# Spectral mixer and MLP on one core: where two transposes, one split, the rest columns, the pair sums and one bias are done

## The chip, the cores and the metric

The kernel runs on one core of one Trainium2 chip. The metric is device microseconds (us) of one execution of the whole program; three executions of the kernel before gave 2691.61, 2695.22 and 2697.30 us, so the median is 2695.22 us. The engines are named as in the profile: PE (TensorE, matmuls), PEld (its weight loads), DVE (VectorE), ACT (ScalarE), POOL (GpSimd) and SP (SyncE, which here only issues DMAs). Each engine executes its own instructions in the order of the program; engines wait for one another by semaphores.

## The reference, cut to what matters

`x` is 2048 x 576, `w1` 576 x 4608 and `w2` 4608 x 576, all float32. Two kinds of layer alternate, twice each.

```python
def A(y):                        # spectral mixing, y = layernorm(x)
    a = y @ dft_hid_re.T
    b = y @ dft_hid_im.T
    return dft_seq_re @ a - dft_seq_im @ b

def B(y):                        # MLP; normalizes y once more inside
    h = gelu(layernorm(y) @ w1 + b1)
    return h @ w2 + b2

x = x + A(layernorm(x))
x = x + B(layernorm(x))
x = x + A(layernorm(x))
x = x + B(layernorm(x))
```

## The kernel before, in words

All matmuls are float32 products made of three reduced-precision passes (`PASSES`): each operand is split into a high part (a copy by ACT into type fp32r) and a low part (operand minus high part, by DVE). `split` (L201 for ACT, L198 for DVE, since every subtraction is recorded at the helper `sub`) does both; names with `high` and `low` do one each. The big products go through a seven-product scheme over 2 x 2 blocks (`ORDER` lists the seven), which needs sums and differences of blocks beforehand.

One layer pair has these stages, in this order.

- **Sequence stage** (`Sequence.run`, from L698). The seq-DFT is done first, on 16 output tiles of 128 rows. The two *plain tiles* come first (`first_mms`, eight block pairs). The other 14 go through the *main loop*: 98 steps of 24 matmuls with 288 columns, seven to a tile. Step n makes, ahead of time, the low part for step n+2 (`low`, DVE) and the high part for step n+3 (`high`, L647, ACT); `sums` makes the next tile's block sums on DVE. After a step `post` combines its PSUM bank. Finished tiles (`uv`, 128 x 1152) are transposed in 32 x 32 blocks on DVE (`turned`, L205) and stored to `uv_mid` in DRAM. In the first layer, `pump` puts pieces of the preparation of `w1` between the steps: loads `in_w`, high parts at L278/L279 (ACT), low parts (DVE), sums (POOL).
- `first_post` (L602) copies the four PSUM banks of a plain tile to SBUF (L606, ACT), transposes it (DVE) and issues its store from ACT's queue (L609), so ACT stands until the transpose is done. For tile 0 this comes straight after `first_mms`, ahead of the main loop's first low part; for tile 1 after step 1.
- During the seven steps of the last tile `Hidden.begin` (L756) prepares the next stage: it issues the loads of the hidden-DFT matrix `dh` (nine blocks) and of the first `uv` tiles (four DMAs each), in the first layer splits the nine blocks (`high_d` L821, `low_d`), and at n == 5 splits the first `uv` tile (`turn(0)`), behind blocks 3 to 5.
- **Hidden stage** (`hidden`, from L871), twice per layer, for 8 tiles each. Tile n is 54 matmuls (9 blocks x 3 passes x 2 halves). Then DVE adds the result to the residual tile (L195), takes its statistics (L223 to L226), and POOL turns these into a scale and an offset (L229, L232, L233: the *moments*). At the start of tile n+1 ACT splits the `uv` tile n+2 (L201) and normalizes tile n (L252) into a buffer `t8` shared by two tiles, and POOL adds the bias `b2` to the residual tile (L195). After every second tile a pair is complete. `rests` copies the last 32 columns of four blocks, three times each, into `es` (L917, three POOL copies). Behind the matmuls of the even tiles 2, 4 and 6 `turn_blocks` transposes a pair on PE: eight 128 x 128 transposes (L931) and four from `es` (L934), copied out of PSUM by ACT (L935, L936). In the next odd tile `turn_sums` splits three blocks (`parts`, L944 and L198) and makes four block sums of 128 x 384 (on POOL for the first two pairs, on DVE for the third); `turn_parts` then splits the four sums.
- **MLP stage** (`mlp`): products with `w1`, gelu, products with `w2`, by the same scheme.

Nothing reorders the work: each engine's queue is the order in which the Python code calls it. SP issues most DMAs, one after the other.

## Time and profile before

| | us |
|---|---|
| median of three executions | 2695.22 (2691.61 to 2697.30) |
| the profiled execution | 2693.01 |
| its span, first to last instruction | 2691.1 |
| PE busy in the span | 2644.4 (98%) |
| ACT busy | 1099.5 (41%) |
| DVE busy | 1819.4 (68%) |
| POOL busy | 850.6 (32%) |

Between the span and the time of the profiled execution lie 1.9 us. A row of the profile's list of groups or of its timeline gives a source line, engine, operation, `out<-in`, shapes of output and input, a count, busy time, and in brackets or behind the last bar the time the engine had been idle before it and what ended that. A row of the timeline merges neighbouring instructions of one line and engine under the shape of the first. All subtractions stand under L198 and all additions under L195.

### The profile page before, as it was taken

How to read it: one execution, taken by the hardware profiler on the slowest of the kernel's cores; microseconds unless marked ns; L12 is line 12 of the kernel's file. 1: busy time of each engine (PE TensorE's matmuls, PEld its weight loads, DVE VectorE, ACT ScalarE, POOL GpSimd, SP SyncE). 2: the span in 40 equal slices, each digit the busy share in tenths (PEclk: the TensorE clock that was granted, in tenths of full speed). 3: DMA queues.
4: the chain of work that ended last, by engine and by line, in shares of the span. 5: the costliest groups of instructions: out<-in, count | busy, mean ns of one | idle time of the engine just before them, and what ended most of it. 6: DMA issues, size and time to landing. Idle time of an engine off the chain costs nothing. (4 is left out here: it accounts for less than half of the span.)

```text
span 2691.1 us, 44720 instructions
## 1 busy us (share of the span) xinstructions
PE 2644.4 (98%) x17252; PEld 2479.6 (92%) x17252; DVE 1819.4 (68%) x2515; ACT 1099.5 (41%) x1773; POOL 850.6 (32%) x766
## 2 busy tenths in 40 slices
PE   9999999999999999999999999999999999999998
PEld 9999998888888988998899999988999999899998
DVE  8999976877777565556667776566555556655555
ACT  6555644544453343333344333343333324433332
POOL 5344335434443532222251000143222235322222
PEclk9999999999999999999999999999999999999999
DMA  5677675777778566666453333646666684766664
GB/s 189 238 263 244 238 259 185 258 267 274 266 278 291 162 187 195 195 217 207 156 209 121 121 121 121 204 132 194 195 191 197 193 265 133 206 193 195 192 194 152
DMA packets 223109, 544.90 MB, mean 202 GB/s; under 512 B 23584, under 2 KB 74784, under 8 KB 222752
## 3 DMA queue, kind: packets, MB, share of 16 engines
q1 hardware_dynamic: 209568, 511.94, 60.1%
q10 hardware_dynamic: 13328, 30.09, 2.9%
q8 instruction: 137, 2.24, 0.3%
q14 instruction: 76, 0.62, 0.1%
HBM read 429.87 MB, written 114.72 MB: 202 GB/s over the span
## 5 line engine op out<-in xcount | busy, mean ns | idle before, releaser
L208 PE MATMUL bank<-R 128*128 128x288 f32 (+2 forms) x16972 | 2613.2, 316 | 21.6 <-DVE R L198 6.3
L208 PEld LDWEIGHTS bank<-R 128*128 128x128 f32 x16972 | 2448.2, 189 | 182.4 <-DVE A L195 16.5
L195 DVE TENSOR_TENSOR A<-bank,A 128x576 f32<-128x576 f32 (+3 forms) x808 | 568.5, 710 | 558.2 <-PE bank L208 471.4
L198 POOL TENSOR_TENSOR R<-A,R 128x512 fp32r<-128x512 f32 (+1 forms) x286 | 373.3, 1316 | 904.6 <-ACT R L1233 877.2
L198 DVE TENSOR_TENSOR R<-A,R 128x1024 fp32r<-128x1024 f32 (+10 forms) x539 | 535.0, 1018 | 81.0 <-ACT R L944 30.7
L195 POOL TENSOR_TENSOR A<-A 128x576 f32<-128x576 f32 (+2 forms) x102 | 155.2, 1524 | 542.5 <-ACT A L687 343.9
L198 POOL TENSOR_TENSOR A<-A 128x384 f32<-128x384 f32 (+3 forms) x184 | 229.3, 1249 | 248.1 <-DVE R L198 102.2
L1172 ACT ACTIVATE bank<-bank,b1t 128x512 f32<-128x512 f32 (+1 forms) x224 | 144.9, 647 | 368.7 <-DVE bank L195 242.7
L1233 ACT ACTIVATE R<-A 128x512 fp32r<-128x512 f32 x288 | 177.0, 629 | 273.2 <-DVE A L198 123.7
L647 ACT ACTIVATE R<-A 128x1024 fp32r<-128x1024 f32 x196 | 206.1, 1053 | 120.1 <-PE bank L208 63.2
L195 DVE TENSOR_TENSOR bank<-bank,A 128x512 f32<-128x512 f32 (+1 forms) x228 | 152.2, 670 | 143.5 <-PE bank L208 142.6
L198 DVE TENSOR_TENSOR R<-bank,R 128x512 fp32r<-128x512 f32 x232 | 156.3, 676 | 4.7 <-ACT R L1233 4.2
L198 DVE TENSOR_TENSOR A<-A 128x1024 f32<-128x1024 f32 (+3 forms) x134 | 143.3, 1076 | 4.5
L1199 ACT ACTIVATE A<-bank 128x512 f32<-128x512 f32 (+1 forms) x76 | 43.7, 575 | 229.1 <-PE bank L208 229.0
L1233 ACT ACTIVATE R<-bank 128x512 fp32r<-128x512 f32 x216 | 121.2, 595 | 30.1 <-PE bank L208 30.1
L198 DVE TENSOR_TENSOR A<-bank,A 128x512 f32<-128x512 f32 x144 | 98.0, 681 | 0.0
L1172 ACT ACTIVATE A<-bank,b1t 128x512 f32<-128x512 f32 (+1 forms) x76 | 50.5, 665 | 66.5 <-DVE bank L195 66.5
L278 ACT ACTIVATE R<-A 128x256 fp32r<-128x256 f32 x126 | 52.0, 413 | 59.1 <-DMA w_parts<-R 21.8
L252 ACT ACTIVATE A<-A,moments 128x576 f32<-128x576 f32 x58 | 48.5, 860 | 52.7 <-POOL moments L233 24.6
L279 ACT ACTIVATE R<-A,power,middle 128x128 fp32r<-128x128 f32 x126 | 60.8, 483 | 0.0
L944 ACT ACTIVATE R<-A 128x768 fp32r<-128x768 f32 (+2 forms) x36 | 32.9, 946 | 56.0 <-POOL A L198 55.9
L205 DVE STREAM_TRANSPOSE A<-A 128x1152 f32<-128x1152 f32 x32 | 44.1, 1378 | 10.9 <-ACT A L606 7.6
(64 smaller groups left out, 601.6 us busy)
## 6 DMA issues: line engine op xcount, KB each, us to landing
R<-w_parts SPq DMA_DIRECT2D x504, 320.0 KB, 3.4
R<-w_parts SPq DMA_DIRECT2D x189, 576.0 KB, 3.7
A<-in_cs SPq DMA_DIRECT2D x112, 512.0 KB, 4.1
w_parts<-R SPq DMA_DIRECT2D x63, 576.0 KB, 5.3
w_parts<-R ACTq DMA_DIRECT2D x81, 320.0 KB, 3.6
uv_mid<-A SPq DMA_DIRECT2D x28, 576.0 KB, 3.0
w_parts<-R SPq DMA_DIRECT2D x45, 320.0 KB, 4.3
A<-in_w SPq DMA_DIRECT2D x72, 192.0 KB, 4.5
```

The source lines that it names most:

```text
L195: engine.tensor_tensor(dst, a, b, op=op)
L198: engine.tensor_tensor(dst, a, b, op=OP.subtract)
L205: nc.vector.transpose(block(2 * D), block(2 * D))
L208: nc.tensor.matmul(o, a, b, start=start, stop=stop, skip_group_check=True)
L252: nc.scalar.activation(dst, src, AF.Identity, bias=mv[:, 4:5], scale=mv[:, 3:4])
L278: nc.scalar.activation(t[:, 1:4:2], src[:, 0:3:2], AF.Copy)
L279: nc.scalar.activation(t[:, 2], src[:, 1], AF.Identity, bias=power[:, 2:3], scale=middle)
L647: nc.scalar.activation(self.cells[t, i](2, NP, P)[:, 0], self.source(t, i), AF.Copy)
L944: nc.scalar.activation(y[:, i, 0:3, at], x, AF.Copy)
L1172: nc.scalar.activation(dst, src, AF.Gelu_apprx_tanh, bias=bias(f))
L1199: nc.scalar.activation(up, o, AF.Copy)
L1233: nc.scalar.activation(H[q, k](2, TC)[:, 0], src, AF.Copy)
```

## The change

Five things change; what is computed stays the same.

- The transpose and store of plain tile 0 move from ahead of the main loop to behind step 1, those of tile 1 from behind step 1 to behind step 3 (`first_turn`). The bank copies stay where they were. The buffers involved are reserved later accordingly.
- In `Hidden.begin` the split of the first `uv` tile (`turn(0)`) and the load behind it move ahead of `high_d`/`low_d` of step 5, and the load of the second `uv` tile moves from step 0 to step 2.
- `rests` for the first three pairs is one ACT copy with 384 elements a partition in place of three POOL copies with 128.
- `turn_sums` runs on DVE for all pairs.
- The addition of `b2` (POOL) is recorded at the fifth block of the next tile instead of straight after the normalization.

```diff
@@ first_post
                     nc.scalar.activation(uv[:, i, 1 - j], banks[4 * (1 - t) + 2 * i + j][:, :DH], AF.Copy,
                                          scale=-1.0 if i else 1.0)
+
+        def first_turn(self, t, out):
             turned(out)
             nc.scalar.dma_start(uvd[t], out(2 * D))
+            clock[0] += 1
+            out.free()
@@ post
-            if i == 1:
+            if i == 2:
                 self.out = A.alloc(2 * D)
@@ run
-            outs[0].free()
-            hidden.reserve()
...
                 if n == 1:
+                    self.first_turn(0, outs[0])
+                    hidden.reserve()
                     self.first_post(1, outs[1])
-                    clock[0] += 1
-                    outs[1].free()
+                if n == 3:
+                    self.first_turn(1, outs[1])
@@ Hidden.begin
-            if n == 0:
-                self.load_uv(0)
-                self.load_uv(1)
+            if n in (0, 2):
+                self.load_uv(n // 2)
...
+            if n == 5:
+                drain(self.turn(0, Block(R, self.first_ut, 2 * KH * P)))
+                self.load_uv(2)
             for k in ((), (), (), (), (0, 1, 2), (3, 4, 5), (6, 7, 8))[n]:
                 self.high_d(k)
                 self.low_d(k)
-            if n == 5:
-                drain(self.turn(0, Block(R, self.first_ut, 2 * KH * P)))
-                self.load_uv(2)
@@ norms
                 normalize(z, tile_x, mv)
-                add(nc.gpsimd, tile_x, tile_x, b2t(2, DH))
...
             yield
+            if n < NP - 1:
+                add(nc.gpsimd, tile_x, tile_x, b2t(2, DH))
+            yield
@@ rests
             if j < 3:
-                for r in range(3):
-                    nc.gpsimd.tensor_copy(es(7, 3, 32)[:, :4, r], v[:, 0:4, 2 * P:])
+                nc.scalar.activation(es(7, 3, 32)[:, :4], v[:, 0:4, None, 2 * P:].to_broadcast([P, 4, 3, 32]), AF.Copy)
                 return
@@ turn_sums
-            g = nc.gpsimd if j < 2 else nc.vector
+            g = nc.vector
@@ hidden, loop over the tiles
             if n:
-                drain(turn(n + 1), *ln)
+                drain(turn(n + 1))
+                next(ln)
...
+                if k == 4:
+                    next(ln, None)
...
-            g = norms(n)
-            next(g)
-            ln = [g]
+            ln = norms(n)
+            next(ln)
```

The order of instructions shows it at three places. First DVE's queue in the first layer, from the last low part of the plain tiles (128x4x288) to behind step 1. `R<-A,R 128x1024` is the low part of a main-loop step, `A<-A 128x1024` a block sum, `A<-bank,A` the `post` of step 1. Before:

```order
L198 TENSOR_TENSOR R<-A,R 128x4x288
L205 STREAM_TRANSPOSE A<-A 128x1152
L198 TENSOR_TENSOR R<-A,R 128x1024
L195 TENSOR_TENSOR A<-A 128x1024
L198 TENSOR_TENSOR A<-A 128x1024 x2
L198 TENSOR_TENSOR A<-A 128x2x288
L198 TENSOR_TENSOR R<-A,R 128x1024
L198 TENSOR_TENSOR R<-A,R 128x4x288
L198 TENSOR_TENSOR R<-A,R 128x1024
L198 TENSOR_TENSOR A<-A 128x1024
L198 TENSOR_TENSOR R<-A,R 128x1024
L195 TENSOR_TENSOR A<-bank,A 128x288
```

And in the changed kernel:

```order
L198 TENSOR_TENSOR R<-A,R 128x4x288
L198 TENSOR_TENSOR R<-A,R 128x1024
L195 TENSOR_TENSOR A<-A 128x1024
L198 TENSOR_TENSOR A<-A 128x1024 x2
L198 TENSOR_TENSOR A<-A 128x2x288
L198 TENSOR_TENSOR R<-A,R 128x1024
L198 TENSOR_TENSOR R<-A,R 128x4x288
L198 TENSOR_TENSOR R<-A,R 128x1024
L198 TENSOR_TENSOR A<-A 128x1024
L198 TENSOR_TENSOR R<-A,R 128x1024
L195 TENSOR_TENSOR A<-bank,A 128x288
L205 STREAM_TRANSPOSE A<-A 128x1152
```

The transpose of tile 0 has moved from ahead of the first low part of the main loop to behind the `post` of step 1. Second, POOL's queue in a hidden stage, from the bias addition of tile 1 (`A<-A 128x2x288`) to the copies of the second pair. Before:

```order
L195 TENSOR_TENSOR A<-A 128x2x288
L917 COPY A<-A 128x4x32 x3
L229 TENSOR_TENSOR moments<-moments,power 128x1
L232 TENSOR_TENSOR moments<-moments 128x1
L233 TENSOR_TENSOR moments<-power,moments 128x1
L195 TENSOR_TENSOR A<-A 128x2x288
L198 TENSOR_TENSOR A<-A 128x384 x4
L229 TENSOR_TENSOR moments<-moments,power 128x1
L232 TENSOR_TENSOR moments<-moments 128x1
L233 TENSOR_TENSOR moments<-power,moments 128x1
L195 TENSOR_TENSOR A<-A 128x2x288
L917 COPY A<-A 128x4x32 x3
```

And in the changed kernel:

```order
L195 TENSOR_TENSOR A<-A 128x2x288
L229 TENSOR_TENSOR moments<-moments,power 128x1
L232 TENSOR_TENSOR moments<-moments 128x1
L233 TENSOR_TENSOR moments<-power,moments 128x1
L195 TENSOR_TENSOR A<-A 128x2x288
L229 TENSOR_TENSOR moments<-moments,power 128x1
L232 TENSOR_TENSOR moments<-moments 128x1
L233 TENSOR_TENSOR moments<-power,moments 128x1
L195 TENSOR_TENSOR A<-A 128x2x288
```

The three copies and the four sums are gone from POOL; the bias addition stands where it stood. The copy stands in ACT's queue straight behind the normalization, and the sums in DVE's queue between `parts` and the residual addition of the odd tile. Third, DVE's queue at steps 4 to 6 of the last tile in the first layer: `R<-R 128x576` is a `low_d` of one `dh` block, `R<-A,R 128x1152` the low part of the split of the first `uv` tile. Before:

```order
L198 TENSOR_TENSOR R<-R 128x576 x3
L198 TENSOR_TENSOR R<-A,R 128x3x128
L195 TENSOR_TENSOR A<-bank,A 128x288
L198 TENSOR_TENSOR R<-R 128x576 x3
L198 TENSOR_TENSOR R<-A,R 128x1152
L198 TENSOR_TENSOR R<-A,R 128x3x128
```

And in the changed kernel:

```order
L198 TENSOR_TENSOR R<-R 128x576 x3
L198 TENSOR_TENSOR R<-A,R 128x3x128
L195 TENSOR_TENSOR A<-bank,A 128x288
L198 TENSOR_TENSOR R<-A,R 128x1152
L198 TENSOR_TENSOR R<-R 128x576 x3
L198 TENSOR_TENSOR R<-A,R 128x3x128
```

The split of the `uv` tile now stands ahead of blocks 3 to 5 instead of behind them.

More of the change, by code (lines that the diff above doesn't have):

```diff
@@ L673, in post @@
             b = banks[4 - 4 * (t % 2) + BANK[i]][:, :DH]
-            if i == 1:
+            if i == 2:
                 self.out = A.alloc(2 * D)
-            uv, (p1, p5, p7) = self.out(2, 2, DH), (self.post_tmp(3, DH)[:, k] for k in range(3))
+            p1, p5, p7 = (self.post_tmp(3, DH)[:, k] for k in range(3))
+            uv = self.out(2, 2, DH) if i not in (1, 6) else None
             u = p1
@@ L988, in turn_y @@
             t8s.give(t8.pop(j))
-        ln = []
+        ln = iter(())
         for n in range(NP):
@@ L1034, in hidden @@
         parts(2, slice(0, 4), slice(3, 7), low=False)
-        drain(g)
+        drain(ln)
         for _ in range(2):
```

## The prediction

> **What bounds the kernel now.** PE is busy 98% of the span, so anything to be gained is in its idle time. I read first who made PE wait (columns: who waited, for whom, us in total, times, longest):
>
> ```profile
> PE bank L934 <- POOL A L917: 15.2, 8, 2.5
> PE bank L208 <- DVE R L198: 6.3, 6, 2.4
> PE bank L208 <- DVE A L195: 5.0, 4, 2.0
> PE bank L208 <- ACT R L647: 2.8, 2, 1.4
> ```
>
> The largest row is the change's first target: the four transposes of `es` (L934) waited eight times, twice in each of the four hidden stages, for POOL's rest copies (L917). The L647 row is the first split of the main loop, once per layer.
>
> Next the granted clock, in windows placed around these waits (columns: window, its length, busy us and instructions of PE, PEld, DVE, ACT, POOL, then granted clock, DMA share and GB/s):
>
> ```profile
> 66.30:69.70 3.40, 1.34 (x8) 1.11 (x9) 2.08 (x2) 2.06 (x3) 2.46 (x2) 1.00 0.01 2
> 69.70:73.10 3.40, 3.40 (x16) 3.40 (x16) 2.38 (x2) 3.40 (x6) 0.00 (x0) 0.51 0.02 5
> 421.30:424.70 3.40, 0.90 (x7) 0.64 (x7) 3.23 (x7) 0.02 (x1) 3.30 (x4) 1.00 0.27 74
> 424.70:428.10 3.40, 3.40 (x15) 3.37 (x16) 0.60 (x1) 3.28 (x4) 0.93 (x3) 0.50 0.92 256
> 2247.40:2250.80 3.40, 3.40 (x17) 3.40 (x15) 1.26 (x1) 3.40 (x5) 0.98 (x4) 0.51 1.02 293
> ```
>
> Windows of 3.4 us at half clock follow windows in which PE was busy for only 1.34 or 0.90 us. There are eight half-clock windows, the first and the last shown; four follow a wait at L934, one each first split, one the end of the first sequence stage, and one a wait late in the first layer that this change doesn't touch. Each loses 3.4 x 0.5 = 1.7 us. So a wait of 2 to 2.5 us is paid nearly twice.
>
> **Hidden stages: rests to ACT, sums to DVE, bias later.** These rows are tiles 3 and 4 of the first hidden stage, for PE, POOL, ACT and DVE (start, busy, engine, line; idle before in brackets):
>
> ```profile
> 406.52 14.63 PE L208 MATMUL bank<-R 128*128 128x288 f32 x108
> 420.99 1.21 PE L931 MATMUL bank<-ident,A 128*128 128x128 f32 x8
> 424.70 1.09 PE L934 MATMUL bank<-ident,A 128*96 128x128 f32 x4 [2.50 <-POOL A L917]
> 403.69 1.43 POOL L195 TENSOR_TENSOR A<-A 128x576 f32<-128x576 f32 x1 [0.98 <-ACT A L252]
> 413.65 4.29 POOL L198 TENSOR_TENSOR A<-A 128x384 f32<-128x384 f32 x4 [1.95 <-DVE R L198]
> 417.90 0.56 POOL L229 TENSOR_TENSOR moments<-moments,power 128x1 f32<-128x1 f32 x1
> 418.80 0.19 POOL L233 TENSOR_TENSOR moments<-power,moments 128x1 f32<-128x1 f32 x1
> 421.35 2.59 POOL L195 TENSOR_TENSOR A<-A 128x576 f32<-128x576 f32 x1 [2.35 <-ACT A L252]
> 423.88 0.76 POOL L917 COPY A<-A 128x128 f32<-128x128 f32 x3
> 417.97 1.49 ACT L944 ACTIVATE R<-A 128x1536 fp32r<-128x1536 f32 x1 [7.06 <-POOL A L198]
> 419.37 1.15 ACT L201 ACTIVATE R<-A 128x1152 fp32r<-128x1152 f32 x1
> 420.42 0.85 ACT L252 ACTIVATE A<-A,moments 128x576 f32<-128x576 f32 x1
> 409.04 4.37 DVE L198 TENSOR_TENSOR R<-A,R 128x1152 fp32r<-128x1152 f32 x5 [1.50 <-ACT R L201]
> 413.99 0.76 DVE L195 TENSOR_TENSOR A<-bank,A 128x576 f32<-128x576 f32 x1 [0.58 <-PE bank L208]
> 414.79 0.82 DVE L223 BATCH_NORM_STATS2 moments<-A 128x6 f32<-128x288 f32 x2
> 419.49 3.19 DVE L198 TENSOR_TENSOR R<-A,R 32x512 fp32r<-32x512 f32 x3 [3.46 <-ACT R L944]
> ```
>
> The chain is long: the sums hold POOL to 417.9; the moments of tile 3 stand behind them and end at 418.99; ACT waits 7.06 us for the sums, then splits them (1.49) and the next `uv` tile (1.15) before it normalizes (0.85, to 421.3); POOL adds the bias (2.59) and only then copies (0.76), to 424.6. PE had begun L931 at 420.99.
>
> The two operations that take over stand elsewhere in the trace (list of groups by shape; mean ns behind the busy time):
>
> ```profile
> L944 ACT ACTIVATE R<-A 128x384 fp32r<-128x384 f32 x12 | 6.1, 511 | 0.0
> L198 DVE TENSOR_TENSOR A<-A 128x384 f32<-128x384 f32 x16 | 8.9, 558 | 0.9
> ```
>
> Now the new order. DVE ends `parts` at 413.4 and does four sums of 0.56, to 415.6; then the residual addition (0.76) and the statistics (414.79 to 416.03 in the trace, 1.2), to 417.6. POOL's moments take 1.1 as before, to 418.7. ACT splits the sums from 415.6 to 417.1, the `uv` tile to 418.3, normalizes from 418.7 to 419.6 and copies the rests in 0.5, to 420.1. PE reaches L934 at about 422.0, so `es` is 1.9 us early. What is late next? The `uv` tile's low part on DVE: 3.19 us behind 417.6, done at 420.8, wanted when PE has ended the transposes at 422.4: 1.6 us early. The fourth engine, POOL, has nothing but moments and bias left; the bias addition waits for nothing new, and nobody waits for it. Over two tiles DVE then has 2 x (0.76 + 1.2) + 4.37 + 3.19 + 2.2 = 13.7 us beside PE's 14.6 + 1.2 = 15.8. It fits, with 2.1 us to spare.
>
> So all eight waits go: 15.2 us, and with them four half-clock windows, 4 x 1.7 = 6.8. **Sum here: -22.0 us.** Bounds: if DVE is late at all eight places by the 1.3 us derived with rival 2, 8 x 1.3 = 10 comes back; more than 22 isn't there to be had.
>
> A rule of the Trainium skill speaks against this part. "SBUF — State Buffer", section "Who interferes with whom", says that a VectorE instruction with two SBUF inputs and a GpSimd instruction that reads SBUF exclude each other, the second waiting for the first to end. The two bias rows above fit that (1.43 us, and 2.59 while DVE was at work). By it a bias addition could hold DVE up by its whole 1.43 us; the slack of 1.6 us still covers that, and two such holds in a row, which it doesn't, are rival 2.
>
> **First split.** DVE's transposes ahead of the main loop in both layers, PE's waits in the first layer, and the first layer's main loop as one window:
>
> ```profile
> 60.00 1.38 DVE L205 STREAM_TRANSPOSE A<-A 128x1152 f32<-128x1152 f32 x1 [2.41 <-ACT A L606]
> 1408.86 1.38 DVE L205 STREAM_TRANSPOSE A<-A 128x1152 f32<-128x1152 f32 x1 [5.22 <-ACT A L606]
> 67.28 0.53 PE L208 MATMUL bank<-R 128*128 128x288 f32 x2 [1.41 <-ACT R L647]
> 68.89 16.39 PE L208 MATMUL bank<-R 128*128 128x288 f32 x110 [1.08 <-DVE R L198]
> 66.00:336.00 270.00, 267.64 (x2010) 267.41 (x2011) 253.81 (x254) 158.92 (x282) 104.91 (x66) 0.99 0.72 245
> ```
>
> DVE stood idle 2.41 and 5.22 us for the bank copies, then transposed for 1.38, and only then made low part and block sums that step 1 is made of. Without the transpose there this starts 3.8 us earlier in the first layer and 6.6 in the second, against a wait of 1.41 + 1.08 = 2.5: the wait goes, and its half-clock window, 4.2 us a layer. ACT's store of the tile, which waited for the transpose ahead of the high part of step 1, goes behind too. Late next in the first layer is DVE itself: it is busy 253.8 of 270 us, and both transposes still have to be done, now at steps 1 and 3. Its whole work moves ahead by the idle time it gave up, 2.4, and PE can't run further ahead than that for long. I take 2.4 of the 4.2 there (bounds 0 and 4.2), in small waits of under 1.7 us. In the second layer no `w1` work stands on DVE, and the store behind a transpose at step 3 delays one high part that ACT makes a step early: 4.2, bounds 2.5 and 4.2. **Sum: -6.6 us.**
>
> **End of the first sequence stage** (first layer only, where `dh` is split). ACT, SP and PE, then DVE's rows that lead to the first two hidden tiles:
>
> ```profile
> 369.81 0.42 ACT L278 ACTIVATE R<-A 128x256 fp32r<-128x256 f32 x1 [8.34 <-DMA A<-in_w]
> 359.97 5.32 SPq L192 DMA_DIRECT2D A<-uv_mid  x8
> 373.15 7.14 PE L208 MATMUL bank<-R 128*128 128x288 f32 x52 [1.21 <-ACT A L685]
> 382.64 17.62 PE L208 MATMUL bank<-R 128*128 128x288 f32 x119 [2.35 <-DVE R L198]
> 379.24 2.08 DVE L198 TENSOR_TENSOR R<-R 128x576 fp32r<-128x576 f32 x3
> 386.80 1.82 DVE L198 TENSOR_TENSOR R<-A,R 128x384 fp32r<-128x384 f32 x2
> 391.10 0.76 DVE L195 TENSOR_TENSOR A<-bank,A 128x576 f32<-128x576 f32 x1 [2.48 <-PE bank L208]
> ```
>
> ACT stood 8.34 us for a weight load that SP issued behind eight `uv` loads (5.32 us); four of them now come later, so it may land up to 2.7 us earlier. That covers the 1.21. The split of the first `uv` tile no longer stands behind three `low_d` (2.08); with the earlier start that covers the 2.35 and its half-clock window. In sight: 1.2 + 2.35 + 1.7 = 5.3. But DVE works without a break up to the split of the second `uv` tile, which ends at 388.6, while PE ended the first hidden tile at 391.1. The second tile can't begin before 388.6 less the earlier start: gain 2.5 with none of it, 5.2 with 2.7. I take 4.0, about the middle. The `uv` load moved to step 2 is wanted only at the split in the first hidden tile. **Sum: -4.0 us.** In the second layer no wait stands there, and none is made: 0.
>
> **Sum of all:** 22.0 + 6.6 + 4.0 = 32.6 us off the profiled execution's 2693.0 gives 2660.4. That execution is 2.2 us below the median of the three, by which it would be 2662.6. I take **2662 us**.
>
> **The rivals.**
> 1. *The half clock isn't caused by the waits.* For it: of eight waits at L934 only four were followed by such a window. Then the waits go, but the six windows counted above (6.8 + 1.7 + 1.7 = 10.2; the first layer's split was taken without one) stay: 2672. Against it: the windows shown follow idle ones directly. In the Trainium skill, "TensorE: Matmul & The Clock Gate", section "HAM oscillation — how this bites in real kernels", the clock falls for idle gaps of over about 3.4 us; by that these waits of 2.5 would be innocent. The trace disagrees so far, with half clock behind 2.5.
> 2. *DVE takes POOL's place in part.* If the sums and the split of the `uv` tile each wait once for a bias addition, DVE is late by 2 x 1.43 less the 1.6 us of slack: 1.3 at eight places, too short for the half clock: +10, 2672. For it: the bias row of 2.59 shows that the two engines do hinder each other. Against it: it was POOL that waited there, not DVE.
> 3. *The first split doesn't gain*, because step 1 is late by another operand (POOL's two subtractions for the last block pair): +6.6, 2669.
> 4. *Slower:* DVE becomes the bound of the hidden stages. Place: the split of the `uv` tile ahead of tiles 5 and 7. If the sums cost on DVE what they did on POOL (4.3 instead of 2.2) and two bias additions each hold it 2.59, its two tiles take 13.7 + 2.1 + 5.2 = 21.0 against 15.8: PE waits 5.2 + 1.7 at eight places, +55, 2717. It decides from 18.2 us on, where 8 x (2.4 + 1.7) eats the 32.6. Against it: the third pair's sums do run at 0.56 on DVE.
>
> **How the numbers follow.** Chances: forecast (2655 to 2668) 0.66, rival 1 0.10, rival 2 0.12, rival 3 0.05, rival 4 0.04, and 0.03 for a milder form of it that comes out level. The forecast's own ends are 2662 less the 1.8 that the first layer's split and the 1.3 that the sequence end may give more, with two half-clock windows (3.4) that fall otherwise, and plus 2.4 and 1.5 for the same places, with one such window (1.7). By itself it holds too little, so the range reaches on to rivals 1 to 3, all at 2669 to 2672, and 2 us beyond for executions that differ: 2655 to 2674, some 8 in 10. A measurement of this kernel can tell some 0.2% (5.4 us) from no change; faster 0.93, same 0.03, slower 0.04.
>
> **What would show it.** The row L934 <- POOL gone, and no L934 <- ACT in its place; at L208 in the hidden stages no new wait on DVE's L198. One or two half-clock windows in place of eight. At 65 us no wait on L647; small waits on DVE between steps 5 and 15 of the first layer. It would be wrong if PE's waits came back under DVE's name at tiles 5 and 7, or if they go and the half clock stays.

## The result and the profile after

The changed kernel takes 2674.18 us (median of four runs, 2670.59 to 2675.68) against 2695.92 of the kernel before (four runs): a ratio of 0.992, 95% interval 0.9903 to 0.9937. It is faster by 22 us (0.8%), not by the 33 that were forecast: 2662 was the predicted time, and 2674.18 lies just beyond the upper end of the range, 2674. The profiled execution took 2675.18 us, its span 2673.3.

First PE's waits in the changed kernel, the four largest rows (who waited, for whom, us in total, times, longest):

```profile
PE bank L208 <- DVE A L195: 7.3, 6, 2.0
PE bank L936 <- ACT A L252: 5.7, 8, 0.8
PE bank L208 <- DVE R L198: 4.0, 7, 1.2
PE bank L208 <- ACT A L1206: 2.0, 5, 0.5
```

The 15.2 us behind POOL's copies (L934 before, L939 now) are gone. In their place stand eight waits of 0.7 us at the transposes ahead of them (L936), for ACT's normalisation (L252). The timeline of the changed kernel at the first of them, for POOL, ACT, DVE and PE:

```profile
416.24 1.04 POOL L229 TENSOR_TENSOR moments<-moments,power 128x1 f32<-128x1 f32 x1 [6.20 <-DVE moments L226]
417.36 0.81 POOL L232 TENSOR_TENSOR moments<-moments 128x1 f32<-128x1 f32 x1
418.25 1.19 POOL L233 TENSOR_TENSOR moments<-power,moments 128x1 f32<-128x1 f32 x1
419.47 0.87 ACT L252 ACTIVATE A<-A,moments 128x576 f32<-128x576 f32 x1 [2.68 <-POOL moments L233]
420.37 0.53 ACT L922 ACTIVATE A<-A 128x384 f32<-128x384 f32 x1
416.19 3.19 DVE L198 TENSOR_TENSOR R<-A,R 32x512 fp32r<-32x512 f32 x3
419.36 0.38 PE L936 MATMUL bank<-ident,A 128*128 128x128 f32 x2
420.39 0.88 PE L936 MATMUL bank<-ident,A 128*128 128x128 f32 x6 [0.65 <-ACT A L252]
```

The rests (L922) cost 0.53 us and nobody waits for them. But the three moments, one number a partition each, take POOL from 416.24 to 419.44: 3.2 us instead of the 1.1 that was put in the sum. They now stand beside three low parts of DVE (416.19, 3.19 us). The second of them by itself, over the whole trace of the changed kernel (shortest, median and longest in ns, then the first and last start):

```profile
L232 POOL TENSOR_TENSOR moments<-moments x28: 193/194/1105, 393.9 to 2248.4; 128x1 f32<-128x1 f32 x28
```

So 0.81 us isn't its own work.

The half clock is gone from the hidden stages. The windows around the first two of these waits, then the two half-clock windows that are left, at 1324 and 1341 us, each behind the window ahead of it (columns as in the prediction: PE's busy time first, the granted clock third from the end):

```profile
420.00:423.40 3.40, 3.01 (x25) 3.02 (x26) 1.49 (x5) 2.90 (x5) 2.31 (x4) 1.00 0.85 189
436.30:439.70 3.40, 2.68 (x23) 2.69 (x23) 1.76 (x5) 2.62 (x4) 2.30 (x4) 1.00 0.83 283
1320.73:1324.14 3.41, 1.39 (x11) 1.16 (x10) 3.41 (x4) 0.63 (x1) 3.02 (x2) 1.00 0.14 25
1324.14:1327.55 3.41, 3.41 (x16) 3.41 (x16) 2.36 (x4) 0.63 (x1) 1.28 (x1) 0.50 0.81 276
1337.80:1341.21 3.41, 1.64 (x13) 1.43 (x12) 3.08 (x5) 0.00 (x0) 0.19 (x1) 1.00 0.96 322
1341.21:1344.62 3.41, 3.41 (x17) 3.41 (x16) 0.76 (x1) 2.89 (x4) 2.56 (x3) 0.50 0.47 194
```

At the first split PE's waits of 1.41 and 1.08 us have become one of 0.20, without a half clock. But a little later, still in the first layer, DVE and ACT stand. The timeline of the changed kernel, PE's row, two of DVE, then ACT's store of tile 1 and what stands behind it in ACT's queue:

```profile
69.52 2.69 PE L208 MATMUL bank<-R 128*128 128x288 f32 x18 [0.20 <-DVE R L198]
78.07 1.37 DVE L205 STREAM_TRANSPOSE A<-A 128x1152 f32<-128x1152 f32 x1
80.73 1.69 DVE L198 TENSOR_TENSOR R<-A,R 128x384 fp32r<-128x384 f32 x2 [1.28 <-ACT R L279]
79.52 0.33 ACTq L611 DMA_DIRECT2D uv_mid<-A  x1
79.89 0.42 ACT L278 ACTIVATE R<-A 128x256 fp32r<-128x256 f32 x1 [2.08 <-issue]
```

ACT can issue the store only when DVE's transpose has ended at 79.44; the weights' high parts (L278, L279) stand behind the store; DVE's next low part needs them. So DVE pays 1.28 us of idle time on top of the 1.37 of the transpose.

To see where the time went, the start of the same matmul in both traces is compared at the ends of the stages. The two profiled executions lie 17.8 us apart, less than the medians do, and the rows add up to that:

| stretch of PE's work | predicted, us | measured, us |
|---|---|---|
| up to the first matmul of the main loop | 0 | 0.0 |
| first layer, main loop | -2.4 | +2.8 |
| end of the first sequence stage | -4.0 | -4.5 |
| first split, second layer | -4.2 | -4.6 |
| four hidden stages | -22.0 | -14.4 |
| all else (the end of the first layer, +1.8, most of it) | 0 | +2.8 |

Two rows make most of the miss: the hidden stages give 7.6 less, and the first layer's main loop loses 2.8 where 2.4 was to be gained.

### The profile page after: what moved, and what is told of

It is laid out like the page before. It is cut to its first block, busy times and chain, and to the rows that moved or that the text cites. A ratio compares the mean times of both kernels' runs of the same rounds, so it can differ in the third digit from the quotient of the medians.

```text
span 2673.3 us, 44719 instructions
## 1 busy us (share of the span) xinstructions
PE 2639.7 (99%) x17252; PEld 2472.7 (92%) x17252; DVE 1836.7 (69%) x2547; ACT 1105.9 (41%) x1785; POOL 814.3 (30%) x698
## 5 line engine op out<-in xcount | busy, mean ns | idle before, releaser
L198 POOL TENSOR_TENSOR R<-A,R 128x512 fp32r<-128x512 f32 (+1 forms) x286 | 373.5, 1317 | 904.5 <-ACT R L1240 865.8
L198 DVE TENSOR_TENSOR R<-A,R 128x1024 fp32r<-128x1024 f32 (+10 forms) x539 | 536.0, 1020 | 61.7 <-ACT R L651 25.3
L195 POOL TENSOR_TENSOR A<-A 128x576 f32<-128x576 f32 (+2 forms) x102 | 148.7, 1461 | 537.0 <-ACT A L692 339.8
L198 POOL TENSOR_TENSOR A<-A 128x288 f32<-128x288 f32 (+3 forms) x152 | 194.1, 1281 | 222.8 <-DVE R L198 90.3
L198 DVE TENSOR_TENSOR A<-A 128x1024 f32<-128x1024 f32 (+3 forms) x166 | 160.3, 970 | 6.2
L198 DVE TENSOR_TENSOR R<-bank,R 128x512 fp32r<-128x512 f32 x232 | 156.3, 677 | 4.8 <-ACT R L1240 4.2
L198 DVE TENSOR_TENSOR A<-bank,A 128x512 f32<-128x512 f32 x144 | 98.1, 681 | 0.0
L278 ACT ACTIVATE R<-A 128x256 fp32r<-128x256 f32 x126 | 52.0, 413 | 64.6 <-DMA A<-in_w 29.3
L252 ACT ACTIVATE A<-A,moments 128x576 f32<-128x576 f32 x58 | 48.6, 861 | 71.5 <-POOL moments L233 43.1
L229 POOL TENSOR_TENSOR moments<-moments,power 128x1 f32<-128x1 f32 x32 | 27.5, 860 | 130.1 <-DVE moments L226 130.1
L279 ACT ACTIVATE R<-A,power,middle 128x128 fp32r<-128x128 f32 x126 | 60.8, 483 | 0.0
```

Of the source, the lines that this page charges most:

```text
L195: engine.tensor_tensor(dst, a, b, op=op)
L198: engine.tensor_tensor(dst, a, b, op=OP.subtract)
L229: nc.gpsimd.tensor_tensor(mv[:, 3:4], mv[:, 2:3], power[:, 0:1], op=OP.pow)
L252: nc.scalar.activation(dst, src, AF.Identity, bias=mv[:, 4:5], scale=mv[:, 3:4])
L278: nc.scalar.activation(t[:, 1:4:2], src[:, 0:3:2], AF.Copy)
L279: nc.scalar.activation(t[:, 2], src[:, 1], AF.Identity, bias=power[:, 2:3], scale=middle)
```

## Experiments

Times are medians of four runs where no other number is given; the kernel before had 2694.57 to 2695.86 in the same sessions. "Gain of the hidden stages" is worked out as in the table: from PE's first transposes in each of the four to its first matmul behind them, against the kernel before.

**Sums back on POOL.** Only this line of the changed kernel differs:

```diff
-            g = nc.vector
+            g = nc.gpsimd if j < 2 else nc.vector
```

> The changed kernel, but the sums of the first two pairs are on POOL again, as in the kernel before; rests stay on ACT, bias stays a tile later. In the changed kernel PE now waits eight times for ACT's normalisation (L936, 5.7 us in total), because POOL's three moments take 3.2 us beside DVE's low parts, where 1.1 was taken. Theory (the moments are hindered by the DVE work that the new order put beside them, and the sums did not have to move): the moments are back near 1.2 us, the normalisation ends at about PE's second or third transpose, the eight waits are 0 to 0.4 us each, and the time is 2 to 5 us less than that of the changed kernel. Rival (sums on DVE are what made the gain): ACT gets the sums 2 us later, the eight waits are as long as in the changed kernel or longer (0.7 us or more each, under L936, L939 or L208 by DVE), and the time is the same or up to 15 us more.

Measured: 2665.10 us, ratio 0.9894 [0.9877, 0.9911]. That is 9.1 less than the changed kernel, more than the theory's 2 to 5. The hidden stages gain 20.5 us, and no wait at L936 is left. At the same place as above:

```profile
415.77 0.56 POOL L229 TENSOR_TENSOR moments<-moments,power 128x1 f32<-128x1 f32 x1
416.41 0.31 POOL L232 TENSOR_TENSOR moments<-moments 128x1 f32<-128x1 f32 x1
416.79 1.16 POOL L233 TENSOR_TENSOR moments<-power,moments 128x1 f32<-128x1 f32 x1
417.98 0.87 ACT L252 ACTIVATE A<-A,moments 128x576 f32<-128x576 f32 x1 [0.99 <-POOL moments L233]
415.98 3.19 DVE L198 TENSOR_TENSOR R<-A,R 32x512 fp32r<-32x512 f32 x3 [2.42 <-ACT R L949]
418.51 1.26 PE L936 MATMUL bank<-ident,A 128*128 128x128 f32 x8
```

Now DVE's low parts begin only when the first moment is under way; two moments take 0.87 us together, and only the last is held (1.16): 2.2 us in all, not the 1.2 of the theory. ACT normalises 0.5 us ahead of PE instead of 0.1 behind it. The rival falls: the sums did not have to move, and their move cost 6.1 us (20.5 less 14.4).

**Two moments on DVE.** The last two of the three moments become one DVE operation behind POOL's power:

```diff
-        nc.gpsimd.tensor_tensor(mv[:, 4:5], mv[:, 0:1], mv[:, 3:4], op=OP.mult)
-        nc.gpsimd.tensor_tensor(mv[:, 4:5], power[:, 2:3], mv[:, 4:5], op=OP.subtract)
+        nc.vector.scalar_tensor_tensor(mv[:, 4:5], mv[:, 0:1], -1.0, mv[:, 3:4], op0=OP.mult, op1=OP.mult)
```

> The changed kernel, but the last two of the three moments of a single tile (product and difference) are one operation on DVE; the power stays on POOL. DVE then waits for the power ahead of its low parts instead of running them beside it. Theory (POOL's moments take 3.2 us because each of them waits for a DVE low part of 1.06 us to end): from DVE's statistics to the normalisation about 1.0 us instead of 2.7, PE's eight waits at L936 (5.7 us in total) shrink to under 0.2 each, and the time is 4 to 5.7 us less than that of the changed kernel; DVE's low parts end 0.7 us later and are still in time. Rival (the moments are slow on POOL by themselves here, or ACT is late by its own work): the normalisation still begins within 0.3 us of where it begins in the changed kernel, and the time is the same within 1 us. Second rival (DVE is late for it): PE's waits move from L936 to L208 by DVE's L198, 0.5 us or more each, and the time is the same.

Measured: 2672.90 us, 1.3 less than the changed kernel where the theory had 4 to 5.7; the hidden stages gain 11.4. The waits at the normalisation are gone, as the theory said, but the second rival took their place: PE waits for DVE's L198 for 8.5 us in all (12 times) instead of 4.0. The timeline of this kernel shows why:

```profile
415.47 0.55 POOL L229 TENSOR_TENSOR moments<-moments,power 128x1 f32<-128x1 f32 x1 [6.20 <-DVE moments L226]
417.19 2.25 POOL L195 TENSOR_TENSOR A<-A 128x576 f32<-128x576 f32 x1 [1.18 <-ACT A L251]
416.05 0.16 DVE L232 SCALAR_TENSOR_TENSOR moments<-moments 128x1 f32<-128x1 f32 x1 [0.66 <-POOL moments L229]
416.24 4.42 DVE L198 TENSOR_TENSOR R<-A,R 32x512 fp32r<-32x512 f32 x3
```

The power alone takes 0.55 us with DVE idle. But the normalisation now comes early, POOL's bias addition follows it at 417.19, and the same three low parts take 4.42 us beside it instead of 3.19: the addition ends at 419.44, and the third low part, begun at 418.08, ends at 420.66 after 2.58 us instead of 1.35. The holding works both ways.

**Shorter DVE operations.** A direct test of the cause: two of the three low parts are cut into halves, so the same work stands beside the moments in shorter pieces.

```diff
-            split(o[:, 0], o[:, 1], v)
+            if n in (5, 7):
+                nc.scalar.activation(o[:, 0], v, AF.Copy)
+                for c in (slice(0, 5), slice(5, KH)):
+                    sub(nc.vector, o[:, 1, c], v[:, c], o[:, 0, c].bitcast(F32))
+            else:
+                split(o[:, 0], o[:, 1], v)
...
-                sub(nc.vector, y[:, i, 3:5, at], x[:, :, 0:2], y[:, i, 0:2, at].bitcast(F32))
+                n = x.shape[1]
+                for c in ([slice(0, n // 2), slice(n // 2, n)] if n == 4 else [slice(0, n)]):
+                    to = slice(i.start + c.start, i.start + c.stop)
+                    sub(nc.vector, y[:, to, 3:5, at], x[:, c, 0:2], y[:, to, 0:2, at].bitcast(F32))
```

> The changed kernel, but two of DVE's low-part operations that stand beside the moments in the hidden stages (1.23 and 1.35 us in the changed kernel) are cut into halves, same work in twice the instructions. Theory (a moment on POOL is held until a DVE operation ends, so its delay is the length of DVE's operations): the three moments take about 2 us from first start to last end instead of 3.2, the normalisation starts about 1 us earlier against PE, PE's eight waits at it (5.7 us in total) fall below 1.5 us in total, and the time is 4 to 5.7 us less than that of the changed kernel. Rival (the moments are slowed by how busy DVE is, not by the length of its operations): moments and waits as in the changed kernel within 0.2 us each, and the time the same or up to 1 us more.

Measured: 2672.11 us. The moments go from 3.20 to 1.99 us (414.82 to 416.81), and the eight waits at the normalisation are gone altogether. Yet the time moved by 2.1 us only: the hidden stages gain 21.8 up to their last transposes, but a new loss of 1.3 us came up at the end of each. There the third pair's low part was cut too, beside POOL's bias addition:

```profile
450.55 1.76 POOL L195 TENSOR_TENSOR A<-A 128x576 f32<-128x576 f32 x1
450.11 2.75 DVE L198 TENSOR_TENSOR R<-A,R 128x512 fp32r<-128x512 f32 x2
```

Whole, this operation took 1.45 us in the changed kernel (453.32 us there) beside the same addition, which then took 2.30. In two pieces it was DVE that was held: 2.75 us, and POOL's addition 1.76. The next run leaves the third pair whole (`n == 4 and j < 2`).

> As the run with the cut low parts, but the low part of the third pair, at the end of a hidden stage, is whole again; its halves took 2.75 us instead of 1.45 beside POOL's bias addition there, and PE waited up to 1.1 us for them. Theory (there DVE was held by POOL, as POOL's moments are held by DVE): the waits of PE at the stage's end (4.8 us for ACT's bank copies in that run) go back to 2.0 as in the changed kernel, the eight waits at the normalisation stay away, the hidden stages gain 5 to 7 us on the changed kernel, and the time is 4 to 7 us less than it. Rival (the cut costs DVE as much as the shorter moments give): waits of PE at L208 for DVE's L198 in the hidden stages, and the time is within 2 us of the changed kernel.

Measured: 2666.22 us, ratio 0.9888 [0.9869, 0.9906]: 8.0 us less than the changed kernel. The hidden stages gain 21.8 us. Its timeline where the changed kernel had 3.2 us of moments:

```profile
412.27 1.05 POOL L229 TENSOR_TENSOR moments<-moments,power 128x1 f32<-128x1 f32 x1 [6.20 <-DVE moments L226]
413.39 0.27 POOL L232 TENSOR_TENSOR moments<-moments 128x1 f32<-128x1 f32 x1
413.74 0.52 POOL L233 TENSOR_TENSOR moments<-power,moments 128x1 f32<-128x1 f32 x1
412.22 3.33 DVE L198 TENSOR_TENSOR R<-A,R 32x512 fp32r<-32x512 f32 x5
415.39 1.04 PE L941 MATMUL bank<-ident,A 128*128 128x128 f32 x8
```

DVE is as busy as ever (3.33 us in five pieces), so it is not how much DVE works that slows the moments, but how long one of its operations lasts. PE's eight transposes start without a wait, and of the 22.0 us of the prediction's term 21.8 are there.

**Rests alone.** The kernel before, with only the three POOL copies replaced by the one of ACT (the `rests` lines of the change).

> The kernel before with one edit alone: the rests are copied by ACT right behind its normalisation, not by POOL behind the bias addition. Sums stay on POOL, the bias stays where it was, the first split too. Theory (only the rests behind POOL's bias made PE wait in the hidden stages; moving the sums to DVE gained nothing and cost 6 us there): the eight waits at the transposes of es (15.2 us) and their four half-clock windows go, PE gains 18 to 21 us over the four hidden stages, and the time is 18 to 21 us less than that of the kernel before. Rival (sums and bias had to move too, for ACT to reach the normalisation in time): waits of 0.5 us or more each come up at the transposes, under ACT's normalisation or its rests, or at L208 under DVE's low parts, and the hidden stages gain 14 us or less, as in the changed kernel.

Measured: 2680.07 us, ratio 0.9945 [0.9930, 0.9960]: 15.7 less than before, between what the theory (18 to 21) and the rival (14 or less) expected. The hidden stages gain 15.5 us, more than the 14.4 of the change. So this one edit carries the whole gain there; sums and bias together added nothing. Four waits are left, at the second pair only (L930 for ACT's L252, 5.3 us, up to 1.4). Here, as in the kernel before, the bias addition right behind the normalisation runs beside five low parts of DVE. The timeline of this run at the first pair, then POOL's second moment between the pairs and PE's wait at the second pair:

```profile
410.93 1.85 POOL L195 TENSOR_TENSOR A<-A 128x576 f32<-128x576 f32 x1 [1.10 <-ACT A L252]
410.13 4.37 DVE L198 TENSOR_TENSOR R<-A,R 128x1152 fp32r<-128x1152 f32 x5 [1.48 <-ACT R L201]
426.42 0.95 POOL L232 TENSOR_TENSOR moments<-moments 128x1 f32<-128x1 f32 x1
439.63 0.88 PE L930 MATMUL bank<-ident,A 128*128 128x128 f32 x6 [1.32 <-ACT A L252]
```

Five operations of the same shapes in the combined kernel below (sums on POOL, stores and bias later):

```profile
420.70 3.35 DVE L198 TENSOR_TENSOR R<-A,R 128x1152 fp32r<-128x1152 f32 x5 [1.35 <-ACT R L201]
```

4.37 us against 3.35: the addition holds DVE for 1.0 us, and the sums behind the low parts begin that much later. At the first pair PE doesn't wait for it yet. But the delay goes on through the moments in between (0.95 us for the second, where it takes 0.19 in the combined kernel) to the second pair, where against PE's transposes the sums begin 2.4 us later than in the combined kernel, and there ACT reaches the normalisation too late.

**First layer: transposes as before.** In the first layer only, tile 0 is transposed ahead of the main loop again and tile 1 at step 1; the second layer keeps the change.

```diff
-            if i == 2:
+            if i == (2 if self.early else 1):
...
+            if not self.early:
+                turned(outs[0])
+                nc.scalar.dma_start(uvd[0], outs[0](2 * D))
...
+            if not self.early:
+                outs[0].free()
+                hidden.reserve()
...
-                    self.first_turn(0, outs[0])
-                    hidden.reserve()
+                    if self.early:
+                        self.first_turn(0, outs[0])
+                        hidden.reserve()
...
-                if n == 3:
+                if n == (3 if self.early else 1):
```

> The changed kernel, but in the first layer the first split is as in the kernel before (transpose of tile 0 ahead of the main loop, of tile 1 at step 1); the second layer keeps the later transposes. In the trace of the changed kernel PE is 4.1 us ahead of the kernel before after the first 3 us of the first layer's main loop, and 2.8 us behind it at the loop's end. Theory (the later transposes in the first layer give back what they gained, and more, through the stores and weight loads behind them): at the end of the first layer's main loop PE stands within 0.7 us of the kernel before, and the time is 2 to 3.5 us less than that of the changed kernel. Rival (the loss within the loop has another cause, such as weight loads that landed late in this one execution): PE starts the loop 4 us later and still loses in it, so the time is 1 to 4 us more than that of the changed kernel.

Measured: 2671.06 us, 3.1 less than the changed kernel, as the theory had it. At the first split PE waits as in the kernel before (1.42 and 1.08 us). From its 500th matmul on it loses nothing more, and it ends the loop 1.2 us behind the kernel before, where the changed kernel was 2.8 behind. That is more than the theory's 0.7: the half clock at the first split lasted 6.8 us in this execution (68.15 to 74.98) and 3.4 in the kernel before. So in the first layer the later transposes gained nothing over the loop, and in the changed kernel's execution they lost.

**First layer: stores later.** The transposes stay where the change put them; only the stores move, so that ACT no longer stands at them.

```diff
-        def first_turn(self, t, out):
-            turned(out)
+        def first_store(self, t, out):
             nc.scalar.dma_start(uvd[t], out(2 * D))
...
                 self.mms(t, i)
+                if n == 2:
+                    self.first_store(0, outs[0])
+                    hidden.reserve()
                 self.post(t, i)
                 if n == 1:
-                    self.first_turn(0, outs[0])
-                    hidden.reserve()
+                    turned(outs[0])
                     self.first_post(1, outs[1])
                 if n == 3:
-                    self.first_turn(1, outs[1])
+                    turned(outs[1])
+                if n == 5:
+                    self.first_store(1, outs[1])
```

> The changed kernel, but the two stores of the turned first tiles are issued by ACT one and two steps after the transposes (steps 2 and 5), not right behind them; transposes are where the change put them. Theory A (in the first layer ACT's queue stands at the store until DVE's transpose has ended, the weight high parts behind it come late, and DVE idles 1.3 us for them, on top of the transpose): that idle time of 1.29 us at 80.7 us goes, DVE is 1.3 us earlier from step 2 on, and PE ends the first layer's main loop 1 to 2.6 us earlier than in the changed kernel. Theory B (the transposes' own 1.38 us each, among steps in which DVE has no slack, cost it): DVE's idle time goes, but PE ends the loop within 0.7 us of where it did in the changed kernel. Theory C (weight loads that land late, 17.0 us of waits of ACT against 7.5 before, are the cause): no change within the loop beyond 0.7 us, and those waits stay at 15 us or more.

Measured: 2667.84 us, ratio 0.9904 [0.9888, 0.9919], 6.3 less than the changed kernel. The same place in its timeline:

```profile
78.18 1.37 DVE L205 STREAM_TRANSPOSE A<-A 128x1152 f32<-128x1152 f32 x1
79.47 2.93 DVE L198 TENSOR_TENSOR R<-A,R 128x384 fp32r<-128x384 f32 x3
76.36 0.41 ACT L278 ACTIVATE R<-A 128x256 fp32r<-128x256 f32 x1
```

The high part comes at 76.36 instead of 79.89, and DVE goes on without a break. Counted from the loop's first matmul, PE gains 3.0 us on the kernel before where the changed kernel lost 2.8: about the 2.4 that the prediction gave to this term, once the store is out of the way. The gain over the changed kernel, 5.8, is more than the 1 to 2.6 of theory A. ACT's waits for weight loads stay (16.4 us against 17.0) while the loop changes, so theory C doesn't hold in the form in which it was put.

How much of the 5.8 us between these two traces is the store? All runs together tell. From PE's 500th to its 700th matmul (some 75 to 102 us) the seven traces with the stores of the change lose 2.55 to 2.61 us on the kernel before, the four with later stores (this one and three below) 1.14 to 1.23. So 1.4 us is the store at this place. From there to the loop's end the seven lose 0.0 to 4.4 us (mean 2.4), the four 0.0 to 2.9 (mean 1.0), and the two with the first split of before nothing. This part differs from execution to execution, and that the store causes it isn't shown. It goes with one late load: DVE waits for an `in_cs` load at 142 to 148 us, 2.41 us in the changed kernel's trace and 0.71 in that of the later stores. In the five traces where this wait is 2.0 to 2.5 us, 1.7 to 4.4 us are lost there, in the four where it is under 0.9, at most 0.6. What makes the load late was not tried.

**Combinations.** First both edits that had gained alone, sums on POOL and stores later:

> The changed kernel with two edits that each gained alone: the sums of the first two pairs on POOL again, and the stores of the turned first tiles issued at steps 2 and 5. Theory (they act in different stages and add up: by the traces 6.2 us in the hidden stages and 4.8 to 5.7 in the first layer's main loop): 10 to 15 us less than the changed kernel, some 2659 to 2664 us. Rival (one of the two was better only in its own executions): the time is that of the better one alone, 2665 to 2668.

Measured: 2666.28 us, ratio 0.9892 [0.9875, 0.9908], which is the rival's number. The hidden stages do gain 20.7 us, so that part adds up; but the profiled execution lost 2.9 us late in the first layer's loop, as described above. The same with the bias straight behind the normalisation, as before the change:

> As the kernel with sums on POOL and later stores, but the bias is added right behind the normalisation again, as before the change, instead of in the middle of the next tile. Theory (in the order with sums on POOL the later bias stands ahead of the moments and costs them 1.3 us, but PE does not wait there any more): moments and normalisation end about 1.3 us earlier against PE, no wait of PE changes, and the time is the same within 1.5 us. Rival (the bias right behind the normalisation holds DVE's low parts up, 4.42 us instead of 3.19 as where both stood side by side): waits of PE at L208 for DVE's L198 at the eight places, 0.5 us or more each, and 4 to 8 us more.

Measured: 2668.54 us, 2.3 more than with the later bias. My theory was wrong: the hidden stages gain only 15.4 us, and four waits at the normalisation are back (5.3 us). The rival had the mechanism (bias beside DVE's low parts), though the wait shows under ACT's name and not under DVE's. So with the sums on POOL the later bias is worth 5.3 us in the hidden stages. With the sums on DVE the edit changes nothing by itself: POOL's queue has the same order with and without it, and in the changed kernel the addition still began right behind the normalisation (at 408.18 us, when ACT's L252 of 407.25 was done) and beside DVE's five low parts, which took 4.38 us. Last, cut low parts and later stores:

> The kernel with the low parts of two pairs cut and, besides, the stores of the turned first tiles issued at steps 2 and 5. Theory: both add up, 5 to 7 us in the hidden stages and 3 to 6 in the first layer's main loop, 8 to 12 us less than the changed kernel, 2662 to 2666 us, level with the kernel that has its sums on POOL and later stores (2666.28 us). Rival (what either gives is lost again to weight loads that land late): 2668 us or more.

Measured: 2665.76 us (2662.17 to 2670.96), ratio 0.9889 [0.9863, 0.9916]: inside the theory's range, but no better than the cut alone. Four kernels now lie between 2665.1 and 2666.3 us, and these runs don't tell them apart. All four beat the changed kernel by 8 to 9 us.

**End of the first sequence stage.** Two runs, one part undone in each (a single execution each, so only the trace is read). First, both `uv` tiles loaded at the first step again:

```diff
-            if n in (0, 2):
-                self.load_uv(n // 2)
+            if n == 0:
+                self.load_uv(0)
+                self.load_uv(1)
```

> The changed kernel, but both first uv tiles of the first hidden stage are loaded at the first step of the last split again, as in the kernel before; the split of the first of them stays where the change put it. From the last matmuls of the first layer's main loop to the first transposes of the first hidden stage the changed kernel gained 4.5 us on the kernel before. Theory (the uv loads stood ahead of a weight load, for which ACT waited 8.3 us before and 5.5 in the changed kernel): ACT's wait is back to 7.5 to 8.5 us, PE waits about 1 us for ACT's bank copy (L690) again, and the gain over this stretch is 1.5 to 3 us. Rival (the loads do not hold each other up; the place of the split alone made the gain): ACT's wait stays at 5 to 6 us, and the gain at 4 to 5.

Second, the three lines at `n == 5` (the split of the first `uv` tile, and the load behind it) moved back behind `high_d` and `low_d`:

> The changed kernel, but the split of the first uv tile stands behind the last three low parts of the stage's weights again (2.08 us of DVE), as in the kernel before; the uv loads stay later. Theory (both parts of the change at this place count: with the earlier weight load alone the split ends about 2.1 us later than in the changed kernel): PE waits 1 to 2.3 us at the first hidden tile for DVE's L198, and the gain over the same stretch (4.5 us in the changed kernel) is 2 to 3.5 us. Rival (the split of the second uv tile sets the start of the second hidden tile, whatever the order of the first): the gain stays at 4 to 5 us.

PE's rows in the timeline of the run with the early loads:

```profile
375.43 7.15 PE L208 MATMUL bank<-R 128*128 128x288 f32 x52 [1.48 <-ACT A L690]
382.93 4.78 PE L208 MATMUL bank<-R 128*128 128x288 f32 x34 [0.35 <-DVE R L198]
```

And in that of the run with the late split:

```profile
381.53 22.84 PE L208 MATMUL bank<-R 128*128 128x288 f32 x158 [2.02 <-DVE R L198]
```

With the loads early ACT's longest wait for the weight load is 8.6 us again (5.5 in the changed kernel), PE waits 1.48, and 2.4 us of the 4.5 are left. With the split late PE waits 2.02 and falls to half clock at 382.5; 1.8 are left. The two losses, 2.1 and 2.7, make up the 4.5 within 0.3: both parts count, and each run shows the wait that the prediction had named for it (1.21 and 2.35 us in the kernel before).

## Why the prediction was right and where it failed

- **End of the first sequence stage** (4.0 forecast, 4.5 measured) and **first split in the second layer** (4.2, 4.6): right, and for the first of them both mechanisms are shown one by one.
- **Half clock**: right. The first rival falls: all four half-clock windows of the hidden stages went with the waits. That the measured 2674 lies near the 2672 of rivals 1 and 2 is chance; the time was lost by other steps.
- **Hidden stages** (22.0, measured 14.4). The step that failed is the sentence "POOL's moments take 1.1 as before, to 418.7". They took 1.1 because DVE stood idle beside them in the kernel before (3.46 us, waiting for ACT). The same paragraph put the `uv` tile's low part on DVE "behind 417.6", so at the same time, and didn't ask what that does to POOL. By the sum the normalisation would have begun 2.3 us ahead of PE's transposes (418.7 against 420.99) and ended 1.4 ahead; it began 0.1 behind them (419.47 against 419.36), and PE waited 0.7 us, eight times. On the matmuls behind them these waits cost 0.7 to 0.9 us each, 6.8 of the 7.6 that are missing. The prediction had looked for a wait under DVE's name at this stage; it came under ACT's. The Trainium skill's rule ("SBUF — State Buffer", "Who interferes with whom") had been read against the bias addition only, in the one direction in which it delays DVE. The Trainium skill says more there: "it's an exclusive lock", and the order of issue decides who blocks. The runs agree with both: where DVE's low parts came first, they took their usual 3.19 us and POOL's moments of 0.19 waited; where POOL's addition came in ahead of the third low part, the three took 4.42.
- **That the sums had to move**: not claimed outright, but the sum was built on it. They didn't: with them on POOL the stages gain 20.5. The move took 4.3 us off POOL ahead of the moments, but it also brought DVE's low parts up to them.
- **First split in the first layer** (2.4 forecast, a loss of 2.8 measured; over the seven traces with the change's stores, from 1.5 gained to 2.8 lost, 0.9 lost in the mean). The waits at the first split did go: PE was 4.1 us ahead at its 500th matmul. The step that failed is "ACT's store of the tile ... goes behind too", which put the cost of the moved store at nothing. The store went behind the transpose, and the transpose went to where ACT's queue holds high parts that DVE needs next: 1.4 us. With the stores one and two steps later the gain was 3.0 in one trace, 2.4 and 2.3 in two others and none in the fourth: the sizing of 2.4 was fair, its condition was missed. That DVE has no slack there was seen; that ACT's queue would pass the wait on was not. The largest part of the loss in the changed kernel's trace, 4.4 us behind the 700th matmul, differs from execution to execution, and its cause stays open.
- **Rival 2** (DVE in POOL's place) did not come about in the changed kernel, but did as soon as the moments were early, in the runs with two moments on DVE and with the third pair cut.
- **Rivals 3 and 4** fall: the first split gained at its own place in both layers, and the four sums took 2.34 us on DVE, not the 4.3 that they had taken on POOL.
- **All else**, +2.8: 1.8 of it is a half-clock window at 1341 us that the trace of before didn't have. The wait ahead of it did stand there before (1.73 us at 1347.9; 1.77 at 1340.2 in the changed kernel), so code that the change left alone led to the half clock in one execution and not in the other.

## What to carry to other kernels

When work moves from one engine to another, ask what it newly stands beside, and not only what it stands behind: a duration read from the trace holds for the neighbour it had there. Tiny operations on GpSimd that hand a value on are best kept away from long two-operand operations on VectorE; if they can't be, cut those, since the delay is one operation's length and not the amount of work. And a DMA issued from a computing engine's queue is a wait on that engine: put its issue some steps behind the work that it waits for.

## What was not expected of the hardware

- Cutting a DVE operation of 1.45 us into two beside a POOL addition made it 2.75 us. The cut shortens POOL's waits and lengthens DVE's, so in these runs it paid only where what stood on POOL was short.
- At the end of the first sequence stage PE waited 1.48 us (loads early) and kept the full clock, and 2.02 us (split late) and lost it. In the changed kernel, windows with 2.68 us of PE's work out of 3.40 stayed at full clock, and those behind 1.39 and 1.64 didn't. In the Trainium skill, "TensorE: Matmul & The Clock Gate", section "HAM oscillation — how this bites in real kernels", gaps of over about 3.4 us are named; here 2.02 was enough.
- The length of a wait alone doesn't decide, though: in the run with sums on POOL a wait of 2.02 us (to 1319.14) kept the full clock, in the first run with cut low parts one of 2.43 (to 863.71). In each trace the half-clock windows begin at whole multiples of 3.413 us from one another (1324.14 and 1341.21 in the changed kernel, 5 x 3.413 apart; 69.73 and 383.76 in the kernel before, 92 x 3.413). Laid on that grid, between 60 and 2600 us of all fourteen traces, the 30 full-clock windows with up to 1.65 us of PE's work were all followed by half clock, those with 1.72 or more never, and of three with 1.69 to 1.71 one was. So a wait costs a half clock where it leaves PE less than about half of one such window. This is also why only four of the eight waits at L934 were followed by one: three of the others were of 0.7 to 1.2 us, and the fourth, of 2.50 (to 1767.86), was split between two windows, which kept 2.61 and 1.71 us of work.
